# Block-sparse attention and a two-layer expert on one core: the layout of v's value tiles, and how the first chunk loads v and the weights

## The chip, the cores and the metric

The kernel runs on one core of a Trainium2 chip. The core has five engines that run their own queues and meet at semaphores: TensorE (PE, products and transposes; its weight loads are listed as PEld), VectorE (DVE), ScalarE (ACT), GpSimd (POOL) and SyncE (SP, which here only issues transfers). Sixteen DMA engines move the data of all queues. The metric is the device time of one execution in microseconds (us).

## What is computed

Attention over 4 batches x 8 heads x 768 positions with heads of 64, in blocks of 32 (24 blocks), and then an expert of two layers. A query block sees the first and the last block of the sequence, itself with its two neighbours, and three sampled blocks; the query blocks 0 and 23 see everything. All in float32:

```python
scores = scale * np.matmul(q, k.transpose(0, 1, 3, 2))
mask = np.abs(blk_i - blk_j) <= window                       # window = 1, in blocks
mask = mask | (blk_i == 0) | (blk_j == 0) | (blk_i == n_blocks - 1) | (blk_j == n_blocks - 1)
for qb in range(n_blocks):
    for kb in sampled_blocks[qb]:
        mask[qb * block:(qb + 1) * block, kb * block:(kb + 1) * block] = True
attn = softmax(np.where(mask, scores, -1e9))
x = (attn @ v).transpose(0, 2, 1, 3).reshape(3072, 512)
out = square(np.maximum(x @ w_in, 0.0)) @ w_out               # w_in 512 x 2048, w_out 2048 x 512
```

## The kernel before, in words

**Tiles and chunks.** A tile is 128 queries of one batch: 4 query blocks (index j, `NJ` = 4) and 8 heads. There are 24 tiles; three tiles (`UC`) are a chunk of 384 tokens, so there are 8 chunks. A tile's attention is done in two halves u = 0, 1 of four heads each (class `Half`), and the query blocks 0 and 23, which see everything, in four `Whole` units per batch, each a pair of heads. The expert of a chunk (`moe`) runs over 16 blocks f of the hidden width: `hidden` (L780) makes the squares, `project` (L810) adds their product with w_out.

**A half.** `scores` (L374, PE), row maxima (L385 and L388, DVE), exponentials (L423, ACT), transposes (`turn`, L437, PE), their copies to SBUF as pT (L446, ACT for the first chunk's tiles), products with the values (`values`, L459, PE) and the normalization into x (L474 to L479, DVE). In the first chunk the four `Whole` units (rows with names g, pg, ptg, pTg, pvg) go before the six halves. When the three tiles are there, `turn(c)` transposes x (xt, L773) and splits it into a rounded part xh (ACT, L776) and the rest xl (DVE, L777); then the first expert product (ph, L788) can begin.

**v in SBUF.** For each query block the values of the eight blocks it sees lie in two tiles of 128 partitions. V0 has on its partitions the first and last block of the sequence ("static", 64 partitions) and two sampled blocks; V1 has the third sampled block and the three neighbours ("window", partitions 32 to 127). Their free axes are (half u, query block j, 260 = 4 heads x 65 numbers; the 65th is a one, which gives the row sum). In DRAM a row of v holds all 8 heads, 520 numbers, so a row's two halves lie side by side there, and in SBUF they are four blocks apart. The three tiles of the first chunk have pairs of their own: `V[0]`, `V[1]`, `V[2]`; all later tiles use `V[0]` again, one half at a time (`halves`).

**How the first chunk gets v.** Tile 0's window is loaded (`load_window`, L304, SP). The windows of tiles 1 and 2 are copied from vn, the whole v of the batch by halves of heads, in copies of one 32 x 260 block (`copy_window`, L217): tile 1's first half by POOL, its second by DVE (list `moves`, one per step from step 22 on), tile 2's 24 by ACT (list `fixed`, one per step from step 7 on). The static part is loaded once and copied within SBUF (`copy_static`, L209, ACT). Sampled blocks are loaded one by one with an index from a register (`load_sampled`, L317, SP), 12 transfers per tile.

**Weights.** Each of the 32 weight blocks comes as 64-bit numbers (craw, 512 KB, L692, POOL's queue), and is made float32 by two passes on ACT (`cut`, L708 and L710) and two on DVE (`cut_bits`, L719 and L720), some of them then split (`cut_split`, L726 and L727). `cut_next` does one step of this pipeline for successive blocks: a load, and five steps later (`AHEAD`) the block's ACT passes, then one step later its DVE passes. Before the first chunk's loop it is called five times in a row, so five loads stand together on POOL's queue; in the loop it is called at step 30 and every fifth step from there (`CUT_0`), in the expert every third step. `need` calls it more often where a block would be too late.

**What sets the order.** The program's order on each engine is that in which the code is run: `Stream` steps the halves as coroutines, a new unit every fifth step (`STEP_0`), with the lags of `LAG_0` between their parts; each step also issues one entry of `fixed`, one of `moves`, one piece of the next keys on POOL (`copy_keys`, L263 and L284). Each engine works its queue in order. Transfers of SP go round eight semaphores, so an issue waits until the one eight before it has landed.

## Time and profile before

| | |
|---|---|
| median of 3 runs | 758.04 us (757.9 to 759.26) |
| profiled execution, span | 757.7 us |
| busy over the span: PE, DVE, ACT, POOL | 733.0, 500.2, 539.4, 502.1 us |
| mean granted TensorE clock | 0.993 |
| transfers | 92434 packets, 97.45 MB |
| PE idle before 57.5 us and after it, to 757 | 47.5 - 36.8 = 10.7 us from 10 us on; 6.8 us |

The profile is of one execution. In its rows a line such as L217 is the source line above; `V<-vn 32x260` says what is written from what, with partitions x elements, and buffer numbers left out. A timeline row begins with the start and the length in us; brackets give the idle time before it on its engine and what ended it. "issue" there means that nothing the profile shows ended it. The granted clock is PE's, as a share of full speed.

### The profile page before, as it was taken

To read this page: it belongs to the slowest core of one execution; us is meant where nothing else is said; L and a number is where in the kernel's file an instruction comes from. 1 tells how busy PE (TensorE), PEld (TensorE's weight loads), DVE (VectorE), ACT (ScalarE), POOL (GpSimd) and SP (SyncE) were. 2 spreads that over 40 slices of the span, in tenths; PEclk is the share of its full clock that TensorE was granted. 3 is DMA by queue.
4 is the path that set the end of the run, shared out by engine and by line. 5 is a ranking of instruction groups with operands and counts; after the bars stand their busy time and mean duration, and the time that the engine had idled before them with its cause. 6 is when DMAs were issued, how large, how long until landed. Compare 5 with 4: busy or idle time off the path is not lost.

```text
span 757.7 us, 26295 instructions
## 1 busy us (share of the span) xinstructions
PE 733.0 (97%) x9832; PEld 612.4 (81%) x9832; DVE 500.2 (66%) x988; ACT 539.4 (71%) x1193; POOL 502.1 (66%) x636
## 2 busy tenths in 40 slices
PE   5779999999999999999999999999999999999997
PEld 2666777678888888888888888887888888888986
DVE  5785785658785756667777575666868666645452
ACT  5896877898876876689786767679876776733222
POOL 6963844237776675757777567666876575777885
PEclk9899999999999999999999999999999999999999
DMA  8776799644443436544434344654344352201001
GB/s 282 217 210 187 223 272 339 136 119 141 125 119 92 144 90 186 153 105 118 119 102 107 98 126 107 225 120 139 84 122 114 81 138 65 51 1 44 1 1 42
DMA packets 92434, 97.45 MB, mean 129 GB/s; under 512 B 14803, under 2 KB 79700, under 8 KB 92308
## 3 DMA queue, kind: packets, MB, share of 16 engines
q1 hardware_dynamic: 86324, 72.80, 36.6%
q0 software_dynamic: 5696, 22.58, 8.8%
q8 instruction: 78, 1.28, 0.7%
q14 instruction: 48, 0.39, 0.2%
q10 hardware_dynamic: 288, 0.39, 0.1%
HBM read 89.43 MB, written 6.29 MB: 126 GB/s over the span
## 4 chain that ended last, share of the span: by engine, by line
PE 84%; DMA 5%; ACT 5%; DVE 3%; issue 1%; SPq 1%; POOL 1%; ACTq 0%; POOLq 0%; DVEq 0%
PE ph L788 33%; PE po L826 30%; PE s L374 7%; PE pv L459 6%; DMA V<-in_v_dram 3%; PE po L816 3%; PE g L546 2%; PE pvg L604 2%; DMA KG<-in_k_dram 1%; PE pt L437 1%; PE xt L773 1%; DVE xl L777 1%; ACT V L209 1%; DMA kn<-in_kn_dram 1%; SPq L317 1%
## 5 line engine op out<-in xcount | busy, mean ns | idle before, releaser
L413 ACT ACTIVATE pm<-p 32x256 f32<-32x256 f32 x576 | 239.2, 415 | 13.2 <-DVE p L391 4.9
L788 PE MATMUL ph<-xh,wi 128*128 128x384 f32 x832 | 237.8, 347 | 0.0
L826 PE MATMUL po<-wo,gh 128*128 128x512 f32 x672 | 213.8, 399 | 0.0
L755 POOL TENSOR_TENSOR wi<-W,wi 128x512 fp32r<-128x512 f32 x104 | 142.2, 1367 | 66.8 <-DVE wi L754 35.2
L806 POOL TENSOR_TENSOR gl<-gf,gh 128x384 fp32r<-128x384 f32 x112 | 117.4, 1048 | 93.3 <-DVE gf L804 80.9
L755 POOL TENSOR_TENSOR wo<-WO,wo 128x512 fp32r<-128x512 f32 x112 | 145.8, 1301 | 49.5 <-DVE wo L754 48.6
L792 ACT ACTIVATE r<-ph 128x384 f32<-128x384 f32 x128 | 63.0, 492 | 161.6 <-PE ph L788 156.5
L804 DVE SCALAR_TENSOR_TENSOR gf<-ph,r 128x384 f32<-128x384 f32 x112 | 62.3, 556 | 150.7 <-ACT r L792 137.1
L788 PEld LDWEIGHTS ph<-xh,wi 128*128 128x128 f32 x832 | 150.4, 188 | 13.4 <-issue 7.4
L826 PEld LDWEIGHTS po<-wo,gh 128*128 128x128 f32 x672 | 123.5, 188 | 23.0 <-issue 2.8
L788 PE MATMUL ph<-xl,wi 128*128 128x384 f32 x416 | 141.4, 340 | 0.0
L826 PE MATMUL po<-wo,gl 128*128 128x512 f32 x336 | 133.1, 396 | 0.0
L754 DVE CAST wo<-WO 128x512 fp32r<-128x512 f32 x112 | 84.3, 753 | 0.0
L788 PEld LDWEIGHTS ph<-xl,wi 128*128 128x128 f32 x416 | 78.2, 188 | 6.9 <-issue 2.9
L826 PEld LDWEIGHTS po<-wo,gl 128*128 128x128 f32 x336 | 63.1, 188 | 15.7 <-POOL gl L806 1.0
L385 DVE TENSOR_REDUCE m<-s 128x2 f32<-128x512 f32 x96 | 61.6, 683 | 10.6 <-PE s L374 10.2
L799 ACT ACTIVATE gh<-r 128x384 fp32r<-128x384 f32 x112 | 59.0, 527 | 9.3 <-ACT r L792 0.4
L459 PEld LDWEIGHTS pv<-V,pT 128*32 128x32 f32 x3072 | 47.2, 109 | 18.9 <-issue 10.5
L459 PE MATMUL pv<-V,pT 128*32 128x65 f32 x3072 | 56.0, 221 | 4.4 <-ACT pT L446 2.3
L788 PE MATMUL ph<-xh,WI 128*128 128x384 f32 x192 | 54.4, 344 | 0.8 <-ACT xh L776 0.8
L374 PE MATMUL s<-KG,q 64*32 64x160 f32 x1536 | 51.3, 307 | 0.6 <-issue 0.3
L418 DVE STREAM_TRANSPOSE pT<-pm 128x1024 f32<-128x1024 f32 x36 | 44.6, 1238 | 4.9 <-ACT pm L413 4.7
(89 smaller groups left out, 933.9 us busy)
## 6 DMA issues: line engine op xcount, KB each, us to landing
craw<-in_w_dram POOLq DMA_DIRECT2D x32, 512.0 KB, 6.0
V<-in_v_dram SPq DMA_DIRECT2D x504, 32.5 KB, 1.8
KG<-in_k_dram SPq DMA_DIRECT2D x216, 64.0 KB, 2.0
V<-in_v_dram SPq DMA_DIRECT2D x28, 390.0 KB, 4.3
q<-in_q_dram SPq DMA_DIRECT2D x24, 256.0 KB, 3.6
out_dram<-ot SPq DMA_DIRECT2D x22, 256.0 KB, 2.6
V<-in_v_dram SPq DMA_DIRECT2D x16, 292.5 KB, 4.0
vn<-in_vn_dram SPq DMA_DIRECT2D x5, 780.0 KB, 6.2
```

The costliest lines, as they stand in the source:

```text
L374: nc.tensor.matmul(self.sb[e][j * BLK : (j + 1) * BLK, i * NSLOT + a : i * NSLOT + z], q[r, j, pr, :], k, start=True, stop=True,)
L385: nc.vector.tensor_reduce(m[:, e], self.sb[e].rearrange("p (i c) -> p i c", i=2), axis=AX, op=ALU.max)
L413: nc.scalar.activation(p[a * BLK : (a + 1) * BLK, j], x[j * BLK : (j + 1) * BLK, :, a], AF.Exp, scale=SCALE)
L459: nc.tensor.matmul(po[j * BLK : (j + 1) * BLK, h * VW : (h + 1) * VW], self.pT[:, j, 2 * e + i, c], v[:, self.u, j, hv : hv + VW], start=( ...
L754: nc.vector.tensor_copy(w[:, 0], src)
L755: nc.gpsimd.tensor_tensor(w[:, 1], src, w[:, 0], op=ALU.subtract)
L788: nc.tensor.matmul(ph[:, :TOK], w, x, start=(i == 0), stop=(i == len(steps) - 1))
L792: nc.scalar.activation(r, ph[:, :TOK], AF.Relu)
L799: nc.scalar.activation(gh, r, AF.Square)
L804: nc.vector.scalar_tensor_tensor(gf, ph[:, :TOK], 0.0, r, op0=ALU.max, op1=ALU.mult)
L806: nc.gpsimd.tensor_tensor(gl, gf, gh, op=ALU.subtract)
L826: nc.tensor.matmul(acc[c][u], g[:, at], w[:, k], start=(f == 0 and i == 0), stop=(f == NF - 1 and i == 2))
```

## The change

The free axes of V0 and V1 become (j, u, 260): the two halves of a row side by side, as in DRAM. Where both halves of a tile are loaded together (the first chunk), one transfer then takes both, with pieces of 520 numbers in place of two times 260. Tile 2's window is loaded by one transfer on SP, ahead of tile 2's sampled blocks; its 24 copies on ACT are gone. Of the five weight loads before the loop two stay where they are, the third goes behind POOL's copies for tile 1, the fourth and fifth behind tile 2's keys. In the loop `cut_next` begins at step 35, not 30. `ACT_TURNS` is a name for the number that stood there.

```diff
-CUT_0 = (30, 5)
+CUT_0 = (35, 5)
...
-ON_ACT = 12
+FIRST_LOADS, SECOND_LOADS = 2, 3
 KEYS_N = 2
+ACT_TURNS = 3
...
-    V = {0: [one.tile([P, 2, NJ, HW // 2], F32, name=f"V{c}") for c in range(2)]}
+    V = {0: [one.tile([P, NJ, 2, HW // 2], F32, name=f"V{c}") for c in range(2)]}
...
     def columns(src, us):
 
-        return src.rearrange("... (u c) -> ... u c", u=2)[..., us, :]
+        n = HW // 2
+        return src[..., us.start * n : us.stop * n]
+
+    def places(v, rows, js, us):
+
+        v = v[rows, js].rearrange("p j u c -> p j (u c)")
+        return columns(v, us)
...
-        for i in range(us.start, us.stop):
-            src = columns(vd[order[k][0], V_STATIC * BLK :], i)
-            src = src.unsqueeze(1).broadcast_to([2 * BLK, n, HW // 2])
-            eng.dma_start(values_of(k)[0][0 : 2 * BLK, i, 0:n], src)
+        src = columns(vd[order[k][0], V_STATIC * BLK :], us)
+        src = src.unsqueeze(1).broadcast_to([2 * BLK, n, src.shape[-1]])
+        eng.dma_start(places(values_of(k)[0], slice(0, 2 * BLK), slice(0, n), us), src)
...
-            for i in range(us.start, us.stop):
-                src = vd[b, (c - 1) * BLK : (c + 1 + n) * BLK, i * HW // 2 : (i + 1) * HW // 2]
-                src = bass.AP(src.tensor, src.offset, [[HW, 3 * BLK], [BLK * HW, n], [1, HW // 2]])
-                eng.dma_start(VB[BLK:P, i, j : j + n], src)
+            src = columns(vd[b, (c - 1) * BLK : (c + 1 + n) * BLK], us)
+            src = bass.AP(src.tensor, src.offset, [[HW, 3 * BLK], [BLK * HW, n], [1, src.shape[-1]]])
+            eng.dma_start(places(VB, slice(BLK, P), slice(j, j + n), us), src)
...
-                dst = VB[0:BLK, us, j] if r == 2 else VA[(2 + r) * BLK : (3 + r) * BLK, us, j]
-                eng.dma_start(dst.unsqueeze(1), v4[:, bass.ds(vals[NRAND * j + r], 1)])
+                at = slice(0, BLK) if r == 2 else slice((2 + r) * BLK, (3 + r) * BLK)
+                dst = places(VB if r == 2 else VA, at, slice(j, j + 1), us)
+                eng.dma_start(dst, v4[:, bass.ds(vals[NRAND * j + r], 1)])
...
-                if e == 0 or self.k < UC:
+                if e == 0 or self.k < ACT_TURNS:
...
-                                v[:, self.u, j, hv : hv + VW],
+                                v[:, j, self.u, hv : hv + VW],
...
     load_q(0, 2, own=begin)
+    load_window(2, 1)
     load_sampled(2, 1, nc.sync, SP)
     windows = {
-        (k, u): [(copy_window, k, u, j, n) for j in range(NJ) for n in range(3)] for k in range(1, UC) for u in range(2)
+        (k, u): [(copy_window, k, u, j, n) for j in range(NJ) for n in range(3)] for k in range(1, 2) for u in range(2)
     }
     for k in range(2):
         deque(copy_keys(0, k), 0)
-    for _ in range(AHEAD):
+    for i in range(AHEAD):
+        if i == FIRST_LOADS:
+            for f, *at in windows[1, 0]:
+                f(*at, nc.gpsimd.tensor_copy)
+        if i == SECOND_LOADS:
+            deque(copy_keys(0, 2, begin), 0)
         cut_next()
-    for k in range(1, UC):
-        if k == 1:
-            for f, *at in windows[k, 0]:
-                f(*at, nc.gpsimd.tensor_copy)
-            deque(copy_keys(0, 2, begin), 0)
     fixed = [(copy_static, k, i) for k in range(UC) for i in range(2)]
-    fixed += windows[2, 0] + windows[2, 1][:ON_ACT]
-    moves = windows[1, 1] + windows[2, 1][ON_ACT:]
+    moves = windows[1, 1]
```

What this does to the queues, at three places. First ACT, from the pT copies of tile 0's first half to those of its second (a name such as pT_0_1 is tile 0, half 1, with the buffer's number; V_125 is tile 2's V1), before:

```order
L446 COPY pT_0_0_815<-pt_0_0_1_787 128x4x4x32
L423 ACTIVATE p_0_1_799<-s_0_1_0_690,m_0_1_796 128x256 x2
L423 ACTIVATE p_0_1_799<-s_0_1_1_691,m_0_1_796 128x256 x2
L217 COPY V_125<-vn_1_137 32x260
L708 ACTIVATE ct_827<-craw_0_360 128x512
L710 ACTIVATE craw_0_360<-craw_0_360,below 128x512
L217 COPY V_125<-vn_1_137 32x260 x4
L446 COPY pT_0_1_970<-pt_0_1_0_906 128x4x4x32
```

And after, the same place and on to the next half's pT copy:

```order
L453 COPY pT_0_0_796<-pt_0_0_1_770 128x4x4x32
L430 ACTIVATE p_0_1_782<-s_0_1_0_675,m_0_1_779 128x256 x2
L430 ACTIVATE p_0_1_782<-s_0_1_1_676,m_0_1_779 128x256 x2
L453 COPY pT_0_1_941<-pt_0_1_0_879 128x4x4x32
L453 COPY pT_0_1_941<-pt_0_1_1_880 128x4x4x32
L430 ACTIVATE p_1_0_892<-s_1_0_0_807,m_1_0_889 128x256 x2
L430 ACTIVATE p_1_0_892<-s_1_0_1_808,m_1_0_889 128x256 x2
L715 ACTIVATE ct_948<-craw_0_358 128x512
L717 ACTIVATE craw_0_358<-craw_0_358,below 128x512
L453 COPY pT_1_0_1114<-pt_1_0_0_1053 128x4x4x32
```

Five block copies are gone between the two, and the first weight block's passes stand one half later; on DVE its two passes move behind the next half's maxima in the same way.

Second, POOL before the loop (craw are weight loads, V_123 is tile 1's V1, KG_407 and KG_401 are tile 2's keys), before:

```order
L692 DMA craw_0_360<-in_w_dram 128x1024
L692 DMA craw_0_362<-in_w_dram 128x1024
L692 DMA craw_0_364<-in_w_dram 128x1024
L692 DMA craw_0_366<-in_w_dram 128x1024
L692 DMA craw_1_368<-in_w_dram 128x1024
L217 COPY V_123<-vn_0_133 32x260 x12
L231 TENSOR_LOAD idx
L284 COPY KG_407<-kn_0_126 128x4x2x64
```

And after:

```order
L699 DMA craw_0_358<-in_w_dram 128x1024
L699 DMA craw_0_360<-in_w_dram 128x1024
L224 COPY V_123<-vn_0_132 32x260 x12
L699 DMA craw_0_374<-in_w_dram 128x1024
L238 TENSOR_LOAD idx
L291 COPY KG_401<-kn_0_126 128x4x2x64
```

Three of the five loads left the group; the last two stand behind the 26 key copies that begin with the last row.

Third, SP at tile 2's loads, after (V_124 and V_125 are tile 2's V0 and V1):

```order
L249 DMA q_2_216<-in_q_dram 128x512
L310 DMA V_125<-in_v_dram 96x4x520
L238 TENSOR_LOAD idx
L324 ISA
L324 DMA V_124<-in_v_dram 32x520
```

The second row is new; the last is the first of the tile's twelve sampled transfers, which was 32x2x260.

## The prediction

> **What bounds the kernel now.** I read the busy time by stretches first (columns: stretch, length, then PE, PEld, DVE, ACT, POOL busy with instruction counts, granted clock, DMA share, GB/s).

> ```profile
> 10.00:57.50 47.50, 36.82 (x1044) 27.70 (x1042) 36.41 (x99) 44.28 (x91) 37.47 (x137) 0.89 0.80 230
> 57.50:85.00 27.50, 26.22 (x321) 19.76 (x321) 19.71 (x33) 20.96 (x42) 14.86 (x30) 1.00 0.66 195
> 85.00:131.00 46.00, 46.00 (x664) 32.30 (x652) 32.31 (x56) 34.87 (x68) 23.14 (x33) 1.00 0.91 290
> 131.00:757.00 626.00, 620.51 (x7823) 530.81 (x7822) 407.91 (x786) 437.96 (x994) 420.84 (x415) 1.00 0.39 104
> ```

> From 57.5 us on PE is busy 26.22 of 27.5, 46.00 of 46.0 and 620.51 of 626: whatever moves the point at which that stretch begins moves the end by as much. Before it lies the first chunk's attention, and there ACT is the fullest engine, 44.28 of 47.5. So the question is how much earlier the first expert product can begin. Next, what ACT does there (groups of ACT between 10 and 58 us: count | busy, mean ns | idle before):

> ```profile
> L217 ACT COPY V<-vn 32x260 f32<-32x260 f32 x24 | 9.7, 405 | 0.4
> L710 ACT ACTIVATE craw<-craw,below 128x512 int32<-128x512 uint16 x6 | 5.1, 858 | 0.0
> ```

> The 24 copies of the third tile's neighbour blocks are 9.7 us of it. Then the order of time on ACT and PE, to see which of them stand on the path (brackets: idle time before, and what ended it):

> ```profile
> 18.12 0.82 ACT L217 COPY V<-vn 32x260 f32<-32x260 f32 x2
> 36.06 0.69 ACT L708 ACTIVATE ct<-craw 128x512 f32<-128x512 f32 x1
> 36.65 0.82 ACT L710 ACTIVATE craw<-craw,below 128x512 int32<-128x512 uint16 x1
> 37.50 1.66 ACT L217 COPY V<-vn 32x260 f32<-32x260 f32 x4
> 39.18 1.07 ACT L446 COPY pT<-pt 128x512 f32<-128x512 f32 x2
> 40.28 1.57 ACT L423 ACTIVATE p<-s,m 128x256 f32<-128x256 f32 x4
> 45.03 1.58 ACT L423 ACTIVATE p<-s,m 128x256 f32<-128x256 f32 x4
> 55.42 1.21 ACT L446 COPY pT<-pt 128x512 f32<-128x512 f32 x2
> ```

> ```profile
> 19.61 0.89 PE L604 MATMUL pvg<-vn,pTg 128*32 128x65 f32 x48 [2.29 <-ACT pTg L592]
> 30.84 0.65 PE L604 MATMUL pvg<-vn,pTg 128*32 128x65 f32 x13 [2.14 <-issue]
> 39.82 1.53 PE L459 MATMUL pv<-V,pT 128*32 128x65 f32 x64 [1.69 <-DVE ct L720]
> 52.75 1.75 PE L459 MATMUL pv<-V,pT 128*32 128x65 f32 x64 [1.34 <-ACT pT L446]
> 57.51 1.53 PE L773 MATMUL xt<-ident,x 128*128 128x128 f32 x12
> ```

> PE waits 2.29, 1.69 and 1.34 us for ACT; for the second the profile names DVE, but ACT's pT copy ran from 39.18 and is what those products read. The 2.14 us before 30.84 are of another kind: they split one product of 48 instructions, with nothing that released them.

> **The change, part by part.** *The 24 ACT copies go* (9.7 us) and *the weights' conversion starts one step of five later*: the pair at 36.06 and 36.65 (1.51 us together, 0.69 + 0.82), its two DVE passes with it. What that gives is not 11 us but what the next engine leaves. That is DVE:

> ```profile
> 24.02 1.29 DVE L385 TENSOR_REDUCE m<-s 128x2 f32<-128x512 f32 x2 [1.27 <-PE s L374]
> 29.62 1.29 DVE L385 TENSOR_REDUCE m<-s 128x2 f32<-128x512 f32 x2
> 32.88 1.20 DVE L217 COPY V<-vn 32x260 f32<-32x260 f32 x4
> 34.98 1.29 DVE L385 TENSOR_REDUCE m<-s 128x2 f32<-128x512 f32 x2 [0.90 <-PE s L374]
> 36.30 0.28 DVE L388 TENSOR_SCALAR m<-m 128x4 f32<-128x4 f32 x1
> 38.28 0.82 DVE L719 SCALAR_TENSOR_TENSOR ct<-ct,craw 128x512 int32<-128x512 int32 x1
> 39.14 0.69 DVE L720 SCALAR_TENSOR_TENSOR ct<-craw,ct 128x512 int32<-128x512 int32 x1
> 39.86 1.29 DVE L385 TENSOR_REDUCE m<-s 128x2 f32<-128x512 f32 x2
> ```

> Step by step. (1) Without the two copies at 18.12 ACT is 0.82 us ahead, so is the PE product at 19.61, and so the first maximum on DVE: 24.02 becomes 23.2. (2) From there to the end of the copies at 34.08 (32.88 + 1.20) DVE has no gap; its twelve copies of the second tile stay. The block moves by the same 0.82: it ends at 33.26. (3) Then DVE waited 0.90 us for scores, which PE had late because of its 2.14 us. I take that stall as gone: it fell into a stretch of full DMA load, while five weight blocks were in flight, of which three now start later. The third maximum then begins at 33.3, not 34.98. (4) From the third maximum to the weights' passes it takes 3.30 us (34.98 to 38.28); those passes now stand behind the fourth maximum, which so begins at 36.6 and is done, 1.5 us on with its scaling, at 38.1. (5) ACT meanwhile: exponentials at 34.9 (third maximum with its scaling, 34.98 to 36.58, is 1.6 us), 1.57; the first weight pair there, 1.51; pT, 1.07: free at 39.1. So the exponentials of the fourth half, at 45.03 before, begin at 39.1: **5.9 us earlier**. (6) From there on ACT's queue has the same work in both, one weight pair or cast after each half up to the pT copies at 55.42, with PE waiting for it, so the 5.9 us reach the transposes at 57.51. (7) I take off 0.4 us for PE at half clock in one of the later rounds (below): 5.5.

> *The transfer that replaces the copies*: 96 partitions x 4 blocks x 2080 B, 0.80 MB, one more DMA on SP ahead of tile 2's twelve sampled transfers. *Halves side by side*: a sampled transfer has 32 pieces of 2080 B, not 64 of 1040 B; no product reads more or less. What it costs SP (the issues; then transfers with KB and median us to landing, V from 36 to 58 us, weights from 0 to 60; then two stretches):

> ```profile
> 37.12 9.66 SPq L317 DMA_DIRECT2D V<-in_v_dram  x12
> 49.87 7.00 SPq L317 DMA_DIRECT2D V<-in_v_dram  x12
> V<-in_v_dram SPq DMA_DIRECT2D x12, 65.0 KB, 3.9
> V<-in_v_dram SPq DMA_DIRECT2D x2, 390.0 KB, 8.1
> craw<-in_w_dram POOLq DMA_DIRECT2D x11, 512.0 KB, 6.7
> 40.00:50.00 10.00, 9.52 (x326) 7.55 (x322) 8.04 (x17) 9.89 (x23) 2.70 (x9) 0.83 0.60 164
> 110.00:120.00 10.00, 10.00 (x156) 6.45 (x155) 6.40 (x13) 7.62 (x15) 5.09 (x8) 1.00 0.97 335
> ```

> Twelve issues with 32 pieces took 7.00 us, twelve with 64 took 9.66: 0.22 us less each, 8 us over the 36. Tile 2's last is issued near 46.8 before, so near 38.8 now, and lands 3.9 us later, 42.7. The new transfer lies ahead of them on the queue: between 2.4 us (at the 335 GB/s of the fullest stretch) and 4.9 us (at the 164 of 40 to 50): 45.1 to 47.6. PE needs them at 52.75 - 5.9 = 46.9. The cover is thin, 1.8 us to -0.7; I take it as covered, since the three weight blocks that start later, 512 KB each, are 1.5 MB, nearly twice its bytes. Behind it on SP wait only those twelve and the next tile's loads, which PE reads after 61 us. If not, the bound above costs up to 0.7.

> *POOL*: the twelve copies of tile 1's blocks go ahead of three of five weight issues.

> ```profile
> 20.28 2.62 POOL L692 DMA_DIRECT2D craw<-in_w_dram  x5
> 22.94 5.23 POOL L217 COPY V<-vn 32x260 f32<-32x260 f32 x12
> ```

> The copies start about 1.57 us earlier (3 of 5 issues of 0.52); tile 2's keys follow by 1.0 us, as one issue stays ahead of them. Nobody waits for either: nothing on PE is ended by POOL in this stage. Cost and gain nothing.

> *One more pair in the next stage*: 1.4 us on ACT and 1.4 on DVE move past 57.5. ACT is busy 20.96 and DVE 19.71 of 27.5 there; idle time of 6.5 and 7.8 covers it. Uncovered it costs 1.4. The ACT_TURNS edit has the value it replaces, so does nothing. Sum: 757.7 - 5.5 = 752.2 for the profiled span; the runs' median, 758.04, lies 0.3 above that span, so **752.5 us**.

> **Rule and row: clock and instruction fetch.**

> ```profile
> 22.00:24.00 2.00, 2.00 (x79) 1.42 (x82) 0.71 (x2) 1.94 (x5) 1.88 (x5) 0.54 0.95 337
> 28.00:30.00 2.00, 0.30 (x3) 0.14 (x4) 1.91 (x5) 1.94 (x6) 1.94 (x8) 1.00 1.05 331
> 32.00:34.00 2.00, 2.00 (x39) 1.62 (x45) 1.89 (x8) 1.16 (x2) 2.00 (x10) 0.50 0.35 99
> 42.00:44.00 2.00, 2.00 (x38) 1.61 (x44) 1.00 (x3) 1.96 (x4) 0.00 (x0) 0.50 0.86 230
> ```

> Three times, after the waits of 2.29, 2.14 and 1.69 us, the granted clock is 0.5, and is not after 1.34. [...]

> **The rivals.** *The stall stays or comes elsewhere.* For it: PE runs faster through its instructions, and the new transfer fills the queues. With it the chain goes by PE: the product ends at 30.7, transposes at half clock to 32.7, pT 33.3, exponentials 34.95, transposes 36, pT 36.7, exponentials 38.3, weight pair 39.8, pT 40.8: 45.03 becomes 40.85, a gain of 4.2, 753.8 us. *Full clock.* Should the first slow stretch vanish, the first scores come 1.0 us sooner or more and DVE's block with them: gain 7, 751.0 us. Against it: the wait of 2.29 shrinks only to about 1.5. *Weights late.* In 85 to 131 DMA is 0.91 busy at 290 GB/s. If that sets the pace, an earlier PE waits there for its weights, the 5.5 us are handed back, and one 0.5 MB block more (1.8 us) eats what is left: 757.5 to 758, no change. Against it: PE has no wait there now. *Slower: tile 2's v late.* If the smaller number of pieces buys nothing, SP's last issue stays at 46.8 and lands at 50.7; with 4.9 us of the new transfer, 55.6. PE needed it at 52.75, so everything behind it comes 2.8 us later: 760.8 us; with 8.1 us, as the 390 KB transfers took, 764. It decides from a landing after 52.75.

> **How the numbers follow.** Forecast 0.43 (own range 751.5 to 753.5), stall 0.29, full clock 0.12, weights late 0.07, v late 0.09. Faster by over 0.2% (1.5 us, about what runs of this kernel can tell from no change) is the first three, 0.84; the same 0.07; slower 0.09. The range leaves out the last two and a little of the edge: 750.5 to 755.8.

> **What would show it.** ACT without rows of the block copies and near 33 us busy before the transposes (44.28 - 9.7 - 1.5); PE's xt near 52, not 57.51; no wait over 1 us for ACT pT before the third tile; tile 2's products not ended by a DMA; PE full behind that, with the same busy time. Wrong if PE's wait there is for V, if xt moves and the end does not, or if the time before xt shrinks by less than 3 us.

## The result and the profile after

The change makes the kernel slower: 763.69 us (median of 20 runs, 761.72 to 768.23) against 758.91 for the kernel before on the same chip (20 runs, 756.87 to 766.34), ratio 1.0056 with an interval of 1.0038 to 1.0075. The forecast was 752.5 us, its range 750.5 to 755.8. The profiled execution of the changed kernel needed 766.86 us, the second longest of the 20, so its rows show more than the usual loss.

The same stretches of the changed kernel, in the columns of the prediction:

```profile
10.00:57.50 47.50, 32.38 (x982) 24.28 (x981) 34.47 (x96) 31.41 (x63) 34.77 (x133) 0.96 0.86 240
57.50:85.00 27.50, 25.84 (x353) 19.34 (x354) 21.07 (x34) 22.40 (x44) 15.56 (x29) 1.00 0.65 190
85.00:131.00 46.00, 46.00 (x667) 32.47 (x666) 32.42 (x55) 34.33 (x66) 24.00 (x37) 1.00 0.92 284
131.00:757.00 626.00, 620.45 (x7817) 530.55 (x7817) 408.76 (x787) 438.27 (x996) 421.12 (x415) 1.00 0.39 104
```

ACT gave up what was forecast: 31.41 us busy in the first chunk, not 44.28. But PE is less busy there, 32.38 for 36.82. The maxima on DVE and then the exponentials on ACT show how far the gain got (timeline rows of the changed kernel):

```profile
32.30 1.29 DVE L392 TENSOR_REDUCE m<-s 128x2 f32<-128x512 f32 x2
...
35.69 1.29 DVE L392 TENSOR_REDUCE m<-s 128x2 f32<-128x512 f32 x2
```

```profile
34.86 1.58 ACT L430 ACTIVATE p<-s,m 128x256 f32<-128x256 f32 x4
...
41.10 1.58 ACT L430 ACTIVATE p<-s,m 128x256 f32<-128x256 f32 x4
...
48.71 1.57 ACT L430 ACTIVATE p<-s,m 128x256 f32<-128x256 f32 x4
...
54.17 1.59 ACT L430 ACTIVATE p<-s,m 128x256 f32<-128x256 f32 x4
```

The last two in the kernel before:

```profile
49.17 1.65 ACT L423 ACTIVATE p<-s,m 128x256 f32<-128x256 f32 x4
...
52.77 1.69 ACT L423 ACTIVATE p<-s,m 128x256 f32<-128x256 f32 x4
```

The third half's exponentials begin 5.4 us earlier than before (40.28), the fourth's 3.9 (45.03), the fifth's 0.5 (49.17), and the sixth's 1.4 us later (52.77). What took it back stands on PE (timeline, brackets: idle time before, and what ended it):

```profile
28.07 0.42 PE L611 MATMUL pvg<-vn,pTg 128*32 128x65 f32 x13 [1.56 <-issue]
...
32.67 0.55 PE L466 MATMUL pv<-V,pT 128*32 128x65 f32 x24 [1.15 <-issue]
...
38.78 0.67 PE L466 MATMUL pv<-V,pT 128*32 128x65 f32 x33 [2.81 <-issue]
...
45.83 0.88 PE L466 MATMUL pv<-V,pT 128*32 128x65 f32 x43 [3.74 <-issue]
...
51.23 0.99 PE L466 MATMUL pv<-V,pT 128*32 128x65 f32 x53 [0.58 <-issue]
```

```profile
PE pv L466 <- issue: 8.3, 4, 3.7
...
PE pvg L611 <- issue: 1.8, 2, 1.6
```

```profile
ACT pT L453 <- PE pt L444: 13.3, 6, 3.6
```

```profile
ACT pT L446 <- PE pt L437: 2.3, 2, 2.1
```

So 10.1 us of waiting stand where 2.14 stood, and ACT waits 13.3 us for PE, not 2.3: the two have changed places. The DMA load of the stretch in which it happens, 30 to 50 us, of the kernel before and then of the changed one (a row of each queue has packets, MB and the share of time that its packets took on the 16 engines; q1 is SP's, q0 has POOL's weight loads, q8 PE's instructions; a share over 1 means that packets overlap; in these 20 us of the changed kernel up to 22 were under way at one time):

```profile
30.00:50.00 20.00, 16.99 (x547) 13.63 (x550) 16.52 (x41) 17.45 (x39) 12.70 (x52) 0.83 0.61 160
q1 hardware_dynamic: 1985, 1.92, 39.2%
q0 software_dynamic: 330, 1.18, 19.8%
q8 instruction: 4, 0.07, 1.4%
craw<-in_w_dram POOLq DMA_DIRECT2D x3, 512.0 KB, 5.6
```

```profile
30.00:50.00 20.00, 12.30 (x448) 9.54 (x434) 13.01 (x32) 11.51 (x27) 12.80 (x54) 0.93 0.97 259
q1 hardware_dynamic: 2018, 2.87, 58.3%
q0 software_dynamic: 624, 2.23, 37.0%
q8 instruction: 4, 0.07, 1.6%
craw<-in_w_dram POOLq DMA_DIRECT2D x4, 512.0 KB, 8.6
```

The change brings 2 MB more into these 20 us: the new transfer of 0.80 MB on one queue, two weight blocks on the other. Over the whole of 20 to 57 us it moves 8.4 MB for 8.0, so most of this was moved here from the 10 us ahead and the 7 us behind. The share goes from 0.61 to 0.97, a weight block takes 8.6 us for 5.6, and PE's fetches fall into the same stretch.

A second loss stands behind the first chunk. PE waits for a tile's last sampled keys, and a stretch of 3.4 us at half clock follows:

```profile
137.77 0.33 PE L381 MATMUL s<-KG,q 64*32 64x160 f32 x2 [3.27 <-DMA V<-in_v_dram]
```

```profile
139.30:142.60 3.30, 3.30 (x8) 1.76 (x7) 3.14 (x6) 0.00 (x0) 0.00 (x0) 0.50 0.34 78
```

The profile names V as the releaser; the operand is KG, whose last transfer was issued at 128.35 and landed at 137.63. In these two profiles the first transposes differ by 1.3 us (58.81, 57.51), and from there to the second chunk's transposes it takes 104.57 us for 98.67: 5.9 more. The rest of the program is the same to 0.3 us (601.7 for 601.5).

### The profile page after: what moved, and what is told of

Read it like the earlier page. It is cut to its first block, busy times and chain, and to the rows that moved or that the text cites. A ratio compares the mean times of both kernels' runs of the same rounds, so it can differ in the third digit from the quotient of the medians.

```text
span 765.1 us, 26268 instructions
## 1 busy us (share of the span) xinstructions
PE 732.1 (96%) x9832; PEld 611.3 (80%) x9832; DVE 502.2 (66%) x988; ACT 529.3 (69%) x1169; POOL 502.2 (66%) x636
## 4 chain that ended last, share of the span: by engine, by line
PE 83%; DMA 5%; ACT 4%; DVE 3%; issue 2%; SPq 1%; POOL 1%; ACTq 0%; POOLq 0%; DVEq 0%
PE ph L795 33%; PE po L833 29%; PE s L381 7%; PE pv L466 6%; DMA V<-in_v_dram 4%; PE po L823 3%; PE g L553 2%; PE pvg L611 1%; PE pt L444 1%; DMA KG<-in_k_dram 1%; PE xt L780 1%; DVE xl L784 1%; ACT V L216 1%; DMA kn<-in_kn_dram 1%; SPq L324 1%
## 5 line engine op out<-in xcount | busy, mean ns | idle before, releaser
L420 ACT ACTIVATE pm<-p 32x256 f32<-32x256 f32 x576 | 239.2, 415 | 13.3 <-DVE p L398 4.9
L392 DVE TENSOR_REDUCE m<-s 128x2 f32<-128x512 f32 x96 | 61.6, 684 | 13.3 <-PE s L381 12.9
L466 PEld LDWEIGHTS pv<-V,pT 128*32 128x32 f32 x3072 | 47.5, 109 | 25.5 <-issue 19.8
L466 PE MATMUL pv<-V,pT 128*32 128x65 f32 x3072 | 56.3, 222 | 10.4 <-issue 8.6
## 6 DMA issues: line engine op xcount, KB each, us to landing
craw<-in_w_dram POOLq DMA_DIRECT2D x32, 512.0 KB, 6.0
```

The costliest lines, as they stand in the source:

```text
L392: nc.vector.tensor_reduce(m[:, e], self.sb[e].rearrange("p (i c) -> p i c", i=2), axis=AX, op=ALU.max)
L420: nc.scalar.activation(p[a * BLK : (a + 1) * BLK, j], x[j * BLK : (j + 1) * BLK, :, a], AF.Exp, scale=SCALE)
L466: nc.tensor.matmul(po[j * BLK : (j + 1) * BLK, h * VW : (h + 1) * VW], self.pT[:, j, 2 * e + i, c], v[:, j, self.u, hv : hv + VW], start=( ...
```

## The experiments

Three theories. (1) The added traffic delays the fetches of PE's instruction blocks, and these now set the pace in the first chunk. Its form 1b: the traffic is no matter, PE simply reaches each block sooner. (2) The larger pieces of v are at fault. (3) The loss is the late key near 137 us, brought by weights that were moved back. The runs, in the order of what they show; "waits" is the sum of PE's waits without a releaser up to 60 us, "to second" the time from the first chunk's transposes to the second's, both in us; a ratio is to the kernel before on the same chip. Medians can be compared only within a group that was timed together: the kernel before needed 761.65 us beside e1 to e4, 760.08 beside e5 to e8, 759.5 beside e9 to e12, 759.09 beside e13 to e16 and 759.38 beside e17 and e18. The ratios are those on record and are not the quotients of the medians (for e1 that would be 1.0005).

| | share 30-50 | waits | transposes | to second | median | ratio (interval) |
|---|---|---|---|---|---|---|
| before, three profiles | 0.61, 0.59, 0.71 | 2.1, 3.4, 2.4 | 57.5, 57.8, 55.9 | 98.7, 103.6, 98.6 | 758.91 | |
| change, three profiles | 0.97, 1.02, 0.95 | 10.1, 7.9, 5.1 | 58.8, 58.9, 56.0 | 104.6, 104.0, 99.2 | 763.69 | 1.0056 (1.0038 to 1.0075) |
| e1 layout only | 0.77 | 4.0 | 58.0 | 104.3 | 762.05 | 1.0021 (0.9998 to 1.0045) |
| e2 layout, transfer | 1.05 | 8.9 | 59.0 | 99.0 | 762.4 | 1.0026 (1.0002 to 1.0051) |
| e3 layout, spread weights | 0.83 | 7.8 | 57.7 | 101.4 | 761.31 | 0.9999 (0.9974 to 1.0025) |
| e4 change, step 30 | 0.97 | 11.8 | 61.6 | 98.8 | 764.42 | 1.0049 (1.0022 to 1.0076) |
| e5 change, 2.3 MB less | 0.63 | 5.3 | 55.5 | 101.1 | 760.01 | 1.0012 (0.9984 to 1.004) |
| e6 change, weights 3 ahead | 0.84 | 8.0 | 57.6 | 99.7 | 760.06 | 0.9988 (0.9967 to 1.0008) |
| e12 as e6, copies on ACT | 0.64 | 2.9 | 56.3 | 99.2 | 759.04 | 0.9991 (0.9972 to 1.0011) |
| e18 before, weights 3 ahead | 0.65 | 0.8 | 56.1 | 98.8 | 758.02 | 0.9968 (0.9943 to 0.9993) |

**The parts of the change.** From the changed kernel: e1 takes back the transfer and the weights' moves, e2 the weights' moves, e3 the transfer, e4 only the step.

```diff
# e1, e2: the first five weight loads together again; e1, e2, e4:
-CUT_0 = (35, 5)
+CUT_0 = (30, 5)
# e1, e3: the transfer out, the 24 copies back on ACT (the part for DVE is empty)
-    load_window(2, 1)
-    moves = windows[1, 1]
+    fixed += windows[2, 0] + windows[2, 1][:ON_ACT]
+    moves = windows[1, 1] + windows[2, 1][ON_ACT:]
```

> The kernel before with the halves of heads side by side alone: sampled transfers in 32 pieces of 2080 B, the third tile's 24 block copies on ACT as before, all five weight blocks issued together. Theory 1 (PE's instruction blocks come late because the new transfer and the later weight blocks fill the DMA queues between 27 and 50 us): nothing of that traffic is here, so PE has one wait without a releaser of about 2 us before the transposes, as before (2.14), ACT is busy 44 us in 10 to 57.5, and the time is that of before, 757.5 to 759.5. Theory 2 (the larger pieces themselves make fetches or PE's reads of v slower): 762 to 764, as with the whole change. Theory 3 (the loss sits behind the first chunk, where the weights moved back make a key transfer late near 137 us): no wait of over 1 us on PE there, 757.5 to 759.5.

> The layout and the one transfer of the third tile's neighbour blocks, but the five weight blocks issued together and the later ones as before. Theory 1, if the 0.80 MB of the transfer are what delays the fetches: waits without a releaser of over 2.5 us at two blocks of instructions, as with the whole change (2.81 and 3.74), first transposes near 58, time 758 to 760. Theory 1, if it takes the weight blocks: one wait of 2 us, transposes near 53, time 753 to 755. Theory 3: no wait for a key near 137 us, so at least 3 us less than the whole change's 763.7.

> The layout and the weight blocks spread and moved back (three of the first five behind POOL's copies, the later ones one step of five later), but the third tile's neighbour blocks copied by ACT and DVE, without the transfer. Theory 1, if the weight blocks in 27 to 50 us delay the fetches: waits without a releaser of over 2.5 us twice before the transposes, which come at 58 to 60 us, since ACT is as full as before. If it takes the transfer: one wait of 2 us and transposes at 56 to 57.5. Theory 3 (weights moved back crowd the keys near 137 us): a wait of about 3 us there and 761 to 764; without it 756 to 759.

> The whole change, but the conversion of the later weight blocks (and with it their transfers) begins at step 30, as before, and not at 35. Theory 1: the same traffic or a little more in 27 to 57 us, so the waits without a releaser stay (9 to 12 us of them on PE up to the transposes) and the transposes are at 58 to 59; what is left is only the late part. Theory 3: one weight block fewer in 57 to 131 us, so the wait of 3.27 us near 137.8 goes, and the time falls by 3 to 5 us to 759 to 761. If theory 3 is wrong, 762.5 to 765.

The layout alone costs little: e1's interval leaves room for up to 0.45%, but e3 has the layout too and is at 0.9999, so theory 2 does not carry the loss. The transfer without the moved weights, and the moved weights without the transfer, bring the waits to 8.9 and 7.8 us: either adds to the load, with a share of 1.05 and of 0.83 in 30 to 50 us for the 0.77 of e1. e2 took longer than the 758 to 760 us expected of it. The waits alone do not make the loss: e3 has 7.8 us of them, its transposes at 57.7 as before, and no longer time. It seems that with ACT as full as before they fall into time in which PE would have waited for ACT (PE's waits for pT and pTg are 3.3 us in e3 and 9.9 in the third profile of before), and that they take what is freed where ACT is relieved. Theory 3 as I had it falls: e4 moves the weights forward again and has no late key, but the same time, with waits of 11.8; and e1 has a late key (2.61 us) with no weight moved.

**The traffic.** e5 takes bytes away and leaves every instruction on PE, ACT and DVE; e6 loads the weights three steps ahead.

```diff
# e5
+            n = 2 * DM // 16 if done in range(2, 7) else 2 * DM
+            if n < 2 * DM:
+                nc.gpsimd.memset(flat[:, n:], 0)
+            nc.gpsimd.dma_start(flat[:, 0:n], wcat[f, part].bitcast(I32)[:, 0:n])
# e6 (tile 2's keys stay behind the third load, now the last before the loop)
-AHEAD = 5
+AHEAD = 3
```

> The whole change, but of the third to seventh weight block only a sixteenth is loaded (the rest is set to zero by POOL, so part of the experts' weights is left out): 2.3 MB less traffic between 27 and 50 us, the same instructions on PE, ACT and DVE. Theory 1 (DMA traffic makes PE's instruction blocks late): the waits without a releaser in the first chunk fall from 10.4 us to 4 us or less, the granted clock aside the transposes come at 53 to 55 us, not 58.8, and the time falls by 3 to 6 us against the whole change. Theory 1b (PE, no longer held up by ACT, simply reaches each block sooner than a fetch takes, whatever the traffic): waits of 8 us or more stay, transposes at 57 to 59, time within 1.5 us of the whole change.

> The whole change, but weight blocks are loaded three steps ahead of their conversion, not five: two blocks (1 MB) leave the stretch from 27 to 50 us and are loaded after 57.5, where the DMA share is 0.65. Theory 1: the waits without a releaser fall from 10.4 us to 5 to 7, transposes at 55 to 57, time 1.5 to 3.5 us below the whole change, unless a weight is late in 85 to 131, which would show as a PE wait for a conversion there and give the gain back. Theory 1b: no change of these waits, time within 1.5 us of the whole change.

The waits of e5 up to 60 us, its load in 30 to 50 us and its first transposes:

```profile
PE pvg L611 <- issue: 2.8, 2, 2.3
PE pv L466 <- issue: 2.5, 3, 1.2
```

```profile
30.00:50.00 20.00, 14.12 (x546) 11.35 (x544) 19.07 (x42) 14.90 (x33) 18.95 (x66) 1.00 0.63 160
```

```profile
55.48 1.53 PE L784 MATMUL xt<-ident,x 128*128 128x128 f32 x12
```

With the load back at 0.63, nearly that of before, the transposes come 3.3 us earlier than in the first profile of the change and the waits are 5.3, not 10.1. But a later profile of the change itself has 5.1 (e17, below), so one profile is weak evidence here; e6 has 8.0, within what the change shows by itself. The medians say more, but not about the first chunk alone: e5 and e6 were timed beside the change (e8) and need 2.9 us less each, and for e6 the intervals of the ratios, 0.9967 to 1.0008 and 1.0011 to 1.0072, do not meet. Yet e6's transposes are no earlier than those of the change, and its edit has a second effect, on the late key: in the four profiles with weights three steps ahead (e6, e11, e12, e18) PE's wait for it is at most 0.76 us, and none of the 36 runs of e6, e12 and e18 needs over 762 us, where 13 of the 69 runs of the kernel before beside them need over 762.5. What carries the claim on fetches is e18, below, and the blocks of all profiles, one by one (last section): under a share of 0.6 the next block has landed 2.2 us after PE enters the one before it, at 0.95 and more after 4.7. In these profiles traffic delays the fetches, as theory 1 says; how much of the median that costs these runs do not show. That PE reaches its blocks sooner (1b) is likely a cause as well: e5 has waits of 5.3 at a load at which the kernel before has 2.1 to 3.4, in one profile.

> Halves side by side, weight blocks spread and loaded three steps ahead, the third tile's neighbour blocks copied by ACT and DVE as before (no transfer): 1.8 MB less traffic in 27 to 57 us than the change, but ACT as full as in the kernel before. Theory A: ACT's 9.7 us of copies fit into time in which PE waits for instructions, transposes at 55 to 57 and 757 to 759.5. Theory B (ACT sets the pace): transposes at 57 to 58, time as before the change.

> The change with weight blocks loaded three steps ahead and the first chunk's conversions, and with them its later weight transfers, begun at step 45 instead of 35: about 2 MB less in 27 to 57 us than the change, loaded after 57.5. Theory A with fetches slowed by traffic: waits without a releaser at 4 to 6 us, transposes at 54 to 56, and 757.5 to 759 if no weight is late in 57 to 131; each weight that is late there shows as a PE wait for ACT or POOL W, wi and gives up to 2 us back. Theory B: transposes at 57 to 59.

e12 is e6 with the copies on ACT again. Its waits up to 60 us:

```profile
PE pv L467 <- ACT pT L454: 2.7, 3, 1.2
...
PE pv L467 <- issue: 2.5, 2, 1.8
```

Its ratio is that of e6: putting 9.7 us of copies on ACT costs nothing, and taking them off bought nothing. e11 (e6 with step 45) went wrong as its last clause feared: PE waits 2.83 us for a converted weight, WO, at 70.35, and it needs 766.1 us (1.0090, 1.0061 to 1.0118). It missed in the first chunk too: at a share of 0.81 in 30 to 50 us its waits are 7.3 us, not 4 to 6, and its transposes come at 58.5, not 54 to 56.

**Who holds the first chunk.** One block of instructions more, and one and a half fewer, in the changed kernel and in the kernel before:

```diff
# e9, e13: behind each product with v of the first chunk
+            for n in range(11 if self.k < UC else 0):
+                nc.tensor.matmul(po[0:BLK, 300:301], self.pT[:, 0, 0, 0], ident[:, 0:1], start=True, stop=True)
# e10, e16
-                    for c in range(2):
+                    for c in range(1 if self.k < UC else 2):
```

> The whole change with 66 products of one column added on PE in the first chunk, 11 behind each of its six products with v (132 matmuls and 132 weight loads: one block of instructions more; nothing reads their result). By the mean of a matmul there (22 ns for 65 columns) they are at most 3 us of PE, which is busy 32.4 of 47.5 us and so could hide them. Theory A (in the first chunk PE goes from block to block at the pace of its instruction fetches, 5.2 us a block by the mean of the changed kernel's seven): the first transposes come 4 to 6 us later, at 63 to 65, and the median rises by as much, to 766 to 769. Theory B (ACT and DVE still set the pace and the waits without a releaser lie in time that would be lost anyway): transposes at 59 to 61, the median within 2 us of the change.

> The whole change with one half of the products with v left out in the first chunk (the second 128 keys of each query block, so the first chunk's attention is incomplete): 192 matmuls and 192 weight loads less, one and a half blocks of instructions; loads, transposes, exponentials and copies stay as they are. Theory A (pace of the fetches): the first transposes come 6 to 8 us earlier, at 51 to 53, and the time falls by as much. Theory B: only the last product's half (0.7 us) and what little of the others stands in the chain, transposes at 57 to 58.5, time within 2 us of the change.

> The kernel before with the same 66 one-column products added (one block of instructions more in the first chunk). If the kernel before is held by ACT there, as the prediction read it: transposes at 57.5 to 59, at most 1.5 us later than in its profile. If it already goes at the pace of its fetches: 61 to 63, as the change did (58.8 to 62.4).

> The kernel before with half of the first chunk's products with v left out (the second 128 keys of each query block): one and a half blocks of instructions less. Held by ACT: transposes at 56.5 to 57.5, since only the last product's half (0.7 us) stands in the chain. At the pace of its fetches: 53 to 55, as the change gained 3.6 us.

The additions decide nothing, since I had mispriced them: the 132 matmuls of one column kept PE busy for 5.12 us, not at most 3, in a row with the products that ACT waits for. The transposes came at 62.4 in the change and 62.2 in the kernel before, 3.6 and 4.7 us behind the first profiles, which PE's own time can explain; the medians were 768.82 and 764.13. The omissions do tell something. The first transposes of e10, and of e16:

```profile
55.24 1.53 PE L780 MATMUL xt<-ident,x 128*128 128x128 f32 x12
```

```profile
55.82 1.53 PE L773 MATMUL xt<-ident,x 128*128 128x128 f32 x12
```

In the change the cut brings 3.6 us against two of its profiles and 0.8 against the third (58.8, 58.9, 56.0); in the kernel before 1.7, 2.0 and 0.1 (57.5, 57.8, 55.9). That is on the side of PE as the one that holds the change and ACT the kernel before, as ACT's 13.3 us of waiting and e12 have it, but with little room; and it does not tell fetches from work, since 3.0 us of PE's products (8.7 to 5.7) went too. The medians were 761.26 (1.0025, 0.9997 to 1.0053) and 760.15 (0.9982, 0.9944 to 1.0020): by the ratios e10 gained some 2.4 us on the change, not the 6 to 8 that theory A asked, and the two intervals overlap. Theory A in its strict form, a pace of 5.2 us a block whatever is in it, falls.

**The late key.** e7 puts the keys first on SP; e8 and e17 are the changed kernel again, e14 and e15 the kernel before.

```diff
-            if step == 1 and self.u == 1 and 2 * UC <= n < len(order):
+            if step == 0 and not self.moved and self.u == 1 and 2 * UC <= n < len(order):
```

> The whole change, but from the seventh tile on the twelve key transfers of a tile stand on SP ahead of the transfers of v for the tile before it, not behind them. Theory 3 (the wait of 3.27 us near 137.8 and the stretch at half clock behind it are the last key transfer, issued behind v at 128.35 and landed 9.3 us later): the wait goes, the second chunk's transposes come 98.7 to 99.5 us after the first's as in the kernel before (104.6 in the change), and the time falls by 3 to 5 us to 758.5 to 761, if v is not late in its place (a PE wait for V in 110 to 140 would show that). If theory 3 is wrong (the wait is a chance of one execution): within 1.5 us of the whole change in the median.

> The changed kernel itself, for a second profile and for times beside those of the other runs here. If the key wait near 137 us belongs to the change: a wait of 2 to 4 us on PE there again and the second chunk's transposes 103 to 105 us after the first's. If it is a chance of one execution: none, 98.7 to 99.5 us. The waits without a releaser before the first transposes: 8 to 11 us again by theory 1 and 1b, transposes at 58 to 60; if they were a chance, 2 to 4 us and transposes at 52 to 54.

> The kernel before itself, a second profile. If the key wait near 137 us belongs to the change: no wait over 1 us on PE there, the second chunk's transposes 98.5 to 99.5 us after the first's. If it comes in executions of both: with some chance a wait of 2 to 4 us. First transposes: 57 to 58 if the first profile was usual, 55 to 56.5 if it was late for its kind (its runs' median is 1.4 us below span plus the 1.75 us that lie around a span in the other runs).

> The kernel before, a third profile, read as e14: first transposes at 57 to 58 or at 55 to 56.5; a key wait near 137 us or none.

> The changed kernel, a third profile. If the late key near 137 us is a chance of single executions of both kernels: with some chance none here, then the second chunk's transposes 98.6 to 99.5 us after the first's and a time of 760 to 762.5; with it 103 to 105 us and 765 to 767. The waits of PE for instructions before the first transposes: 7 to 11 us, transposes at 58 to 60, as in both profiles so far.

e7 moves the wait: the keys are issued by 112.3 (the tenth of the twelve has landed at 114.41), v is late instead (2.4 us of PE's waits near 131), and the median is 770.59 (1.0124, 1.0090 to 1.0158), though its profiled execution needed 762.08. e8 repeats the change: 762.94 (1.0041, 1.0011 to 1.0072), with the late key again (2.73 us up to 137.22, half clock from 138.06). But the second profile of the kernel before has it too:

```profile
135.73 0.33 PE L374 MATMUL s<-KG,q 64*32 64x160 f32 x2 [2.90 <-issue]
```

Again KG, with its last transfer issued at 127.16, and 764.49 us. The third profiles of both have none and need 757.59 and 758.26 us. e16, which differs from the kernel before only in the first chunk, has it as well (3.55 us). So the late key is an event of single executions of both kernels, worth about 5 us, and not a property of the change alone. How often each has it I cannot say from three profiles. The waits of the change without it, up to 60 us:

```profile
PE pv L466 <- issue: 4.2, 2, 3.4
...
PE pvg L611 <- issue: 0.9, 1, 0.9
```

Even in this execution, the fastest of the change seen (the lowest of its 32 timed runs, in the result and in e8, is 759.97), its transposes at 56.02 are no earlier than those of the third profile of before (55.92).

**Less traffic in the kernel before.** The one-line edit of e6, and nothing else of the change:

> The kernel before with weight blocks loaded three steps ahead of their conversion, not five, and nothing else: 1 MB less traffic from 20 to 57 us. If the traffic makes the one wait for instructions near 28 us there (2.14, 3.41 and 2.43 us in three profiles): it falls below 1 us, transposes come at 54 to 55.5, and the time falls by 1 to 2.5 us against before (ratio 0.997 to 0.999), unless a weight is late behind 57.5. If ACT alone holds that stage: transposes at 55.5 to 57.5, ratio 0.999 to 1.001.

758.02 us against 759.38, ratio 0.9968 with an interval of 0.9943 to 0.9993: the one run here whose whole interval lies under the kernel before, if barely. In 22 to 32 us the DMA share is 0.76, where three profiles of before had 0.95 to 0.99, and the wait for instructions that ends there is 0.83 us, where they had 2.1 to 3.4, as expected:

```profile
29.53 0.42 PE L604 MATMUL pvg<-vn,pTg 128*32 128x65 f32 x13 [0.83 <-issue]
```

The transposes, though, come at 56.08, not at 54 to 55.5: 1.4 us earlier than in the first profile of before, and no earlier than in its third. Where the rest of the gain lies is open; the late key may be part of it, since none of these 12 runs needs over 760.6 us and 4 of the 17 beside them need over 762.5.

## Why the prediction was wrong, point by point

*ACT and DVE, steps (1) to (4): right but for the stall.* The third maximum came at 32.30 (forecast 33.3), the fourth at 35.69 (36.6), ACT's busy time was 31.4 (33). They came sooner than forecast: the first slow stretch of PE, 20.4 to 23.8 us before, is not in the profile of the change, and the first maximum came at 21.73, not 23.2. That is the condition of the rival "full clock"; its gain did not follow. Two of the three profiles of the kernel before have no such stretch either.

*Step (3), "I take that stall as gone": the first error.* It stayed (1.56 us at 28.07). The reason I gave, three of five weight blocks that start later, is the reason for what followed: they start later, into 27 to 45 us, together with the new transfer, and four more waits came there.

*Step (5): 5.9 us forecast, 3.9 found.* The third half's exponentials came at 34.86 for 34.9, but by luck: the maximum was there 1.0 us sooner, and ACT's pT copy ahead of them, at 33.90, had waited 2.18 us for PE. The fourth's came at 41.10, not 39.1, since the pT copy ahead of them waited for PE behind the 2.81 us.

*Step (6), "so the 5.9 us reach the transposes": the step that failed.* I let ACT's queue set the pace to the end and gave PE none of its own. In its place the runs showed PE waiting for its instruction blocks, 10.1, 7.9 and 5.1 us in three profiles, and ACT waiting 13.3 us for PE. Behind the 3.74 us the lead was 0.5 us, at the transposes -1.3 in the first profile and nothing in the best against the best. Up to the fourth half most of the gain did come through; from there new waits on PE used it up. They are not all of it: in the third profile, with 5.1 us of them, ACT still waits 11.0 us for PE, which ran at half clock for 10.2 us of that chunk. How the time divides between fetches and clock isn't shown, nor why the median rose by 4.8 us and did not merely stay (below).

*The rival "the stall stays or comes elsewhere"* (0.29) named the mechanism and what speaks for it, and was mis-sized: I priced one wait at 1.3 us of the gain, 753.8 us. The waits came to 5 to 10 us, and of the gain of 4.2 us that the rival still had nothing was left. PE's blocks should have been walked through one by one: seven of them lie between 20 and 55 us, and a fetch under the load quoted for 28 to 30 us had cost 6.7 us from block to block (24.17 to 30.84). With two or three of those behind the fourth maximum, most of the 5.9 us was gone; that is an estimate, and worked out after the result.

*The gap of 2.14 us.* I had put it among the rows, at a DMA share of 1.05, and then left it out of the sum, on the ground given in step (3), that fewer weight blocks would be in flight there. The changed kernel has five waits of that kind, of 0.6 to 3.7 us.

*The rest.* Tile 2's last v was issued at 40.68 (38.8) and landed at 47.86 (45.1 to 47.6); PE did not wait for it, being late itself. The pair moved past 57.5 is covered, as forecast: ACT 22.40 and DVE 21.07 of 27.5. Half clock came once (3.4 us) in the first chunk in the first profile of the change, not three times; its other two profiles have 10.2 us of it each, as the first of the kernel before. "Weights late" in 85 to 131 did not happen; PE is busy 46.00 of 46.0. The sum's base was off as well: in the runs here a time lies 1.7 to 1.8 us above its span (766.86 over 765.1), so by that estimate the span of 757.7 belongs to an execution of some 759.4 us, not to the median of 758.04, and its transposes at 57.51 were late for that kernel (55.92 in the execution of 757.59).

*What stays open.* The medians differ by 4.8 us. In the first chunk the change is 0.8 us behind in the mean of three profiles each (57.9 for 57.1), and anything from 1.8 ahead to 2.9 behind by single ones; a late key costs about 5 us where it comes, in two profiles of three for one of three. That would make 2.5 us together, on numbers too small to carry it, and the six profiles are not of usual executions: those of the change are of 766.86, 766.28 and 758.26 us. The timed runs say that more than now and then a late key is at work: the fastest of 20 is 761.72 us, that of the kernel before beside it 756.87. Whether the change has the late key more often, and where the rest of the 4.8 lies, isn't settled.

## What to carry to other kernels

Before an engine is relieved, ask what the next one can do at most, and count among its limits its own instruction fetches: here, at a DMA share of 0.95 and more, the next block of 256 instructions had landed 4.7 us after PE entered the one before it, for 2.2 us at a share under 0.6, and waits without a releaser that cut products 256 instructions apart, 0.6 to 3.7 us each, were the sign. Work that is replaced by a transfer is paid for in the queues (e2, with the transfer, has a share of 1.05 in 30 to 50 us, e1, without it, 0.77), and a transfer that is moved out of one crowded stretch is to be followed to where it lands. One profile is one execution: two more of each kernel would have shown that 2 us of the first chunk, and a wait of 3 us later on, come and go by themselves.

## What the runs showed of the hardware

Over the 20 profiles of this study I took the 155 blocks of PE's instructions that it entered between 19 and 65 us, placed by counting 256 instructions, and their 16 KB fetches from the DMA records. From the entry into one block to the landing of the next, with the DMA share of that time:

```
DMA share meanwhile   blocks   to landing, mean us   PE's wait, mean us
under 0.6               30            2.2                  0.1
0.6 to 0.8              27            2.9                  0.2
0.8 to 0.95             44            3.7                  0.5
0.95 and more           54            4.7                  1.7
```

It is not the place in the program that makes the difference: in the 16 profiles whose PE instructions are the same, one and the same block, entered at 31 to 36 us, takes 2.2 us to the landing of its successor at a share under 0.8 (9 profiles) and 4.9 at 0.95 and more (6). The packet itself took 0.9 to 1.6 us throughout; what grows is the time until it starts, from 1.2 to 3.5 us in the mean of the first and the last row, and up to 5.8. Where PE had waited more than 0.8 us it went on 1.2 to 1.6 us after the landing (51 cases). Why the start is late no run here shows.

I had also not expected that an edit which loads the weights 3 steps ahead and not 5 costs almost nothing in 85 to 131 us, where the load is 0.91: PE is busy 45.75 of 46.0 there in e18.
